# Gated layer's last two token blocks: Strassen products in the way down for five of six groups, with sums of its weights kept in DRAM

## Chip, cores and metric

One Trainium2 chip, one core. The metric is the device time of one execution in microseconds. Three runs of the kernel before took 2135.84, 2137.84 and 2135.84 us; their median is 2135.84.

## What is computed

Three layers one after another, on 4 x 576 = 2304 tokens of width 512: attention with a mask by blocks of 64 keys, a gated layer, and a layer of eight experts whose router is normalised over rows and columns in turn.

```
x = attention(q, k, v)                        # 4 batches, 8 heads, 576 tokens, 64 a head
xn = x / sqrt(mean(x*x) + 1e-6) * rms_g
g, val = xn @ w_gate, xn @ w_val              # 512 -> 1536
x = (g * sigmoid(g) * val) @ w_out            # 1536 -> 512: the way down
P = router(x)                                 # 8 rounds of row and column normalisation
out = sum over e of P[:, e] * (relu(x @ w1[e]) @ w2[e])
```

## The kernel before

**Numbers.** A float32 operand is held as two fp32r tiles, its rounded value and the rest; a product takes three matmuls (`THREE`, line 1234: high by high, high by low, low by high). A weight tile `w` is [128, 2, 512] for that reason, 512 KB. `W` (line 418) is a ring of nine of them; a tile is loaded over an old one when the last product on the old one is through.

**Blocks.** The tokens stand in five blocks, 512, 512, 512, 384, 384 wide (`BL`). `moe1` (line 1347) interleaves blocks 0, 1 and 2 of the gated layer with attention (`groups`): a group `g` is 256 of the 1536 inner columns, and there are six. Block 0 turns the raw weights into pairs and writes them to DRAM (`kept`); later blocks load those.

**Blocks 3 and 4** are the function `middle` (line 1618). They are treated as the two halves of a Strassen-Winograd scheme: `up` (line 1522) makes the gate, then the value, of a group with seven products in place of eight, each six matmuls of 384 columns. For that it needs sums and differences of quarters of two weight tiles, which `fold` (line 1328) makes: two `join`s (high plus low, 512 columns), four additions of 256 columns, and for each of two results a copy and a subtraction that split it again. For nine of twelve pairs (`PRE`, line 1322) this is done while block 2 runs and the two results go to DRAM (`folded`); the other three are folded inside `middle`. `gate` and `val` (lines 1610, 1627) apply the gate; `val` also splits its result into a pair.

**The way down** is `moe1_down` (line 1301): for each of the two blocks four products, one for each 128 output columns, each of 2 x 3 matmuls into a fresh bank of the ring `DN` (three PSUM banks). VectorE adds a bank into the accumulator `accb` (line 1318; in group 0 ScalarE copies, line 1315). The two weight tiles come by line 1640.

**Order.** Nothing is issued directly: every step is an `Op` of a `Graph` with engine, estimated duration and buffers. `emit` (line 136) lists them by a planner: a forward pass by priority, `ROUNDS` backward and forward passes, then random changes of keys (`move`) by the seeds in `MOVES`, and a last forward pass. A step with `alts` goes to the engine that the planner expects to end first, with a `margin` against the second choice. `replay` places filler matmuls (line 88) where it expects PE to be idle. The result is one fixed order for each engine; SP's is the order of the DMA issues.

## Time and profile before

| | before |
|---|---|
| median of three runs | 2135.84 us |
| the profiled execution's own time | 2134.63 us |
| its span | 2132.8 us |
| PE busy | 2110.2 us, 99% |
| VectorE (DVE) busy | 1514.5 us, 71% |
| GpSimd (POOL) busy | 1172.3 us, 55% |
| ScalarE (ACT) busy | 969.3 us, 45% |
| DMA | 414.39 MB, mean 194 GB/s |

How to read it: times are microseconds unless marked ns, counted from the span's start. PE is the matmul engine, PEld its weight loads, SP the queue that issues DMAs. A table by stretches gives for each engine the busy time and, after x, the number of instructions, then PE's granted clock as a share, the share of time in which the DMA engines were busy, and GB/s. A row of a group of instructions reads: line, engine, operation, tile written and tiles read (buffer numbers left out), shapes, count; then the busy time in all and the mean ns of one; then the idle time of the engine just before them and who ended it. A row of waits gives who waited for whom, the total, how many times, and the longest. A row of the timeline gives start and length of a merged run of like instructions. Matmuls overlap, so the distance from start to start, not the length, is the time of one. Filler matmuls and other full float32 matmuls leave two records for each instruction.

### The profile page before, as it was taken

The numbers are of one execution on the slowest core, as the hardware profiler recorded it, in microseconds if no ns is written. First come the engines' busy times: TensorE is split into PE (matmuls) and PEld (weight loads), VectorE is DVE, ScalarE is ACT, GpSimd is POOL, SyncE is SP. The second block draws the span as 40 slices with busy tenths as digits, with TensorE's granted clock in tenths as the row PEclk, the third lists the DMA queues.
The fourth block names the chain that finished last, engine by engine and source line by source line (L and its number), as shares of the span: only waits on it lengthen the run. The fifth ranks groups of instructions, "written<-read, shape, count | busy, mean of one in ns | idle before, by whom it ended". The sixth has DMA issues, their size and how long they took to land.

```text
span 2132.8 us, 31222 instructions
## 1 busy us (share of the span) xinstructions
PE 2110.2 (99%) x10810; PEld 1821.8 (85%) x10810; DVE 1514.5 (71%) x2643; ACT 969.3 (45%) x2098; POOL 1172.3 (55%) x1073
## 2 busy tenths in 40 slices
PE   9899999999999999999999999999999999999999
PEld 7678778888999999999999999999888888888887
DVE  8889887878567875655555555555767776777777
ACT  6679776664435433333433433443433233332332
POOL 5476524677447755555555555553656464564644
PEclk9999999999999999999999999999999999999999
DMA  6678855567654655554454444444656556565553
GB/s 188 183 210 257 277 169 185 187 220 247 208 177 148 230 190 185 193 183 178 179 181 179 178 178 178 178 178 168 242 203 215 182 196 213 191 217 191 196 202 113
DMA packets 168834, 414.39 MB, mean 194 GB/s; under 512 B 28298, under 2 KB 63562, under 8 KB 168676
## 3 DMA queue, kind: packets, MB, share of 16 engines
q1 hardware_dynamic: 168676, 412.39, 57.1%
q8 instruction: 85, 1.39, 0.3%
q14 instruction: 73, 0.60, 0.1%
HBM read 261.24 MB, written 150.53 MB: 193 GB/s over the span
## 4 chain that ended last, share of the span: by engine, by line
PE 90%; DVE 5%; ACT 2%; DMA 1%; POOL 1%; issue 1%; SPq 0%; DVEq 0%; POOLq 0%; ACTq 0%
PE pm L94 53%; PE ps L94 30%; PE po L94 5%; DVE mn L739 1%; PE ps L98 1%; ACT p L746 1%; DVE ptl L928 0%; DVE qa L665 0%; DMA w<-kg 0%; ACT pth L927 0%; DVE acc L1318 0%; DVE acc L506 0%; DVE xx L894 0%; DMA rd<-acc 0%; DVE ka L450 0%
## 5 line engine op out<-in xcount | busy, mean ns | idle before, releaser
L94 PE MATMUL ps<-xs,w 128*128 128x384 f32 (+2 forms) x2613 | 527.9, 345 | 0.0
L94 PEld LDWEIGHTS ps<-xs,w 128*128 128x128 f32 x2613 | 459.5, 188 | 43.5 <-ACT w L446 0.6
L94 PE MATMUL pm<-x,w 128*128 128x512 f32 (+2 forms) x1743 | 420.2, 375 | 1.0 <-POOL x L459 1.0
L94 PEld LDWEIGHTS pm<-x,w 128*128 128x128 f32 x1743 | 305.7, 189 | 50.1 <-POOL x L459 1.3
L1832 DVE SCALAR_TENSOR_TENSOR acc<-pm,Pm,acc 128x512 f32<-128x512 f32 x280 | 209.8, 750 | 130.1 <-PE pm L94 129.9
L459 POOL TENSOR_TENSOR w<-raw,w 128x512 fp32r<-128x512 f32 (+1 forms) x150 | 195.4, 1307 | 171.1 <-ACT w L446 150.8
L94 PE MATMUL pm<-w,h 128*128 128x512 f32 x1152 | 279.8, 391 | 0.0
L94 PE MATMUL pm<-h,w 128*128 128x512 f32 (+1 forms) x1068 | 248.8, 378 | 0.2 <-ACT x L446 0.2
L94 PEld LDWEIGHTS pm<-w,h 128*128 128x128 f32 x1152 | 210.1, 188 | 39.4
L94 PEld LDWEIGHTS pm<-h,w 128*128 128x128 f32 x1068 | 194.1, 188 | 29.9 <-issue 0.6
L94 PE MATMUL pm<-w,x 128*128 128x512 f32 x768 | 187.8, 392 | 0.0
L1550 DVE TENSOR_TENSOR pad<-ps,pad 128x384 f32<-128x384 f32 (+2 forms) x154 | 81.3, 528 | 142.2 <-ACT pad L1545 92.4
L94 PEld LDWEIGHTS pm<-w,x 128*128 128x128 f32 x768 | 142.8, 188 | 26.5
L94 PE MATMUL pm<-xs,w 128*128 128x256 f32 (+2 forms) x699 | 146.9, 334 | 0.0
L1956 DVE TENSOR_TENSOR acc<-pm,acc 128x512 f32<-128x512 f32 x169 | 115.8, 686 | 43.7 <-PE pm L94 40.1
L1545 ACT ACTIVATE pad<-ps 128x384 f32<-128x384 f32 (+2 forms) x142 | 68.3, 481 | 163.7 <-PE ps L94 159.3
L459 POOL TENSOR_TENSOR x<-pad,x 128x512 fp32r<-128x512 f32 (+1 forms) x68 | 95.4, 1405 | 75.8 <-ACT x L446 75.8
L94 PEld LDWEIGHTS pm<-xs,w 128*128 128x128 f32 x699 | 119.9, 189 | 14.2
L446 ACT ACTIVATE w<-raw 128x512 fp32r<-128x512 f32 (+1 forms) x184 | 107.5, 589 | 49.3 <-DMA raw<-w_dram 13.3
L94 PE MATMUL ps<-x,w 128*128 128x256 f32 (+1 forms) x627 | 114.2, 303 | 0.0
L459 POOL TENSOR_TENSOR h<-pad,h 128x512 fp32r<-128x512 f32 (+1 forms) x49 | 66.0, 1352 | 67.1 <-ACT h L446 63.1
L94 PEld LDWEIGHTS ps<-x,w 128*128 128x128 f32 x627 | 97.7, 190 | 1.8 <-issue 0.8
(385 smaller groups left out, 3794.9 us busy)
## 6 DMA issues: line engine op xcount, KB each, us to landing
raw<-w_dram SPq DMA_DIRECT2D x128, 256.0 KB, 3.3
w<-ko SPq DMA_DIRECT2D x36, 512.0 KB, 4.7
w<-kv SPq DMA_DIRECT2D x33, 512.0 KB, 4.6
fa<-w SPq DMA_DIRECT2D x32, 512.0 KB, 2.6
fc<-w SPq DMA_DIRECT2D x32, 512.0 KB, 2.7
fd<-w SPq DMA_DIRECT2D x32, 512.0 KB, 5.0
sb<-w SPq DMA_DIRECT2D x32, 512.0 KB, 4.0
sd<-pad SPq DMA_DIRECT2D x32, 512.0 KB, 2.7
```

Of the source, the lines that this page charges most:

```text
L94: return self.tensor.matmul(**k)
L98: return self.tensor.transpose(**k)
L446: nc.scalar.activation(out=out_(), in_=in_(), func=AF.Copy, scale=scale)
L459: eng.tensor_tensor(out=out_(), in0=a(), in1=b(), op=ALU.subtract)
L739: return A("DVE", t_v1(n), lambda: nc.vector.tensor_reduce(out=m()[a:z, col : col + 1], in_=ps()[a:z, o : o + n], axis=AX, op=ALU.max, neg ...
L746: A("ACT", t_act(n, True, 2), lambda: nc.scalar.activation(out=p()[a:z, c0 : c0 + n], in_=ps()[a:z, o : o + n], func=AF.Exp, bias=m()[a:z, ...
L1545: G.op("ACT", t_act(n, True), lambda: nc.scalar.activation(out=t()[:, 0:n], in_=bank()[:, 0:n], func=AF.Copy), r=[bank], w=[t])
L1550: G.op("DVE", t_v1(n), lambda: nc.vector.tensor_tensor(out=t()[:, 0:n], in0=bank()[:, 0:n], in1=t()[:, 0:n], op=ALU.add), r=[bank, t], w=[t])
L1832: G.op("DVE", 63 + t_v1(512), lambda y=y, dst=dst, tt=tt, e=e: nc.vector.scalar_tensor_tensor(out=dst(), in0=wide(y()), scalar=Pm()[:, tt, ...
L1956: G.op("DVE", t_v1(N), lambda: nc.vector.tensor_tensor(out=dst(), in0=bank()[:, 0:N], in1=dst(), op=ALU.add), r=[bank, dst], w=[dst])
```

## The change

Five parts, with lines of the kernel before.

1. `PRE` now holds all twelve pairs, so no fold is left in `middle`.
2. For groups 0 to 4 the way down takes seven products in place of eight (`down3`), each in two tiles of 128 output columns and three matmuls of 384. Products go in the order 0, 1, 5, 4, 6, 2, 3 into three banks X, Y, Z; a bank that has been read out is not cleared but takes the next product on top, and VectorE adds each reading into the accumulator it belongs to: 14 readings a group. Group 5 keeps `moe1_down`.
3. The right operands are sums and differences of the four results of a group (`operands_h`: four differences, seven splits into pairs, where before four results were split). They stand in a ring of seven (`hl`), and the way down of a group is put after the value of the next.
4. The sums of the down weights are folded while block 1 runs and written to DRAM (`put`, ten tiles); `ld` loads four tiles for a group's way down, one of them half.
5. The planner's constants (`ROUNDS` 14 to 8, `RATE` 260 to 300, smaller margins in `fold`) and the table `MOVES` are new, and with them the order of all engines throughout.

```diff
-ROUNDS = 14
+ROUNDS = 8
-MARGIN, LAND, RATE = 0.0, 2000.0, 260.0
+MARGIN, LAND, RATE = 0.0, 2000.0, 300.0
 MOVES = (
-    21000002, 21000013, 21000024, 21000031, 21000032, 21000033, 21000062, 21000067, 21000082, 21000086, 21000126,
+    34000023, 34000042, 34000043, 34000044, 34000058, 34000071, 34000078, 34000127, 34000149, 34000151, 34000155,
...
-    PRE = {('g', 1), ('g', 4), ('g', 0), ('g', 3), ('v', 2), ('g', 2), ('v', 1), ('g', 5), ('v', 0)}
+    LAST = NF // 2 - 1
+    PRE = {(a, g) for a in "gv" for g in range(NF // 2)}
...
-    def fold(w0, w1_, rr, prio):
+    def fold(w0, w1_, rr, prio, down=False):
...
-        add(256, a22, a21, a22, r=[r1], w=[r1], **k)
-        add(256, a21, a11, a21, op=ALU.subtract, r=[r0, r1], w=[r1], **k)
-        add(256, a11, a22, a11, op=ALU.subtract, r=[r0, r1], w=[r0], **k)
-        add(256, a12, a12, a11, op=ALU.subtract, r=[r0], w=[r0], **k)
+        a12, a21 = (y, x) if down else (x, y)
+        for out, a, b, op in ((a22, a21, a22, ALU.add), (a21, a11, a21, ALU.subtract), (a11, a22, a11, ALU.subtract), (a12, a12, a11, ALU.subtract)):
+            add(256, out[0], a[0], b[0], op=op, r=[*{id(z[1]): z[1] for z in (out, a, b)}.values()], w=[out[1]], prio=prio, margin=300.0)
...
+                if j == 1 and g < LAST:
+                    put("o", g, fold(*pend[3], [RAW.next(), RAW.next()], 0.5, down=True))
...
+        def operands_h(h):
...
+            (b11, b12), (b21, b22) = h
+            ops = {0: split(b11), 1: split(b21)}
+            t1 = diff(DTB.next(), b12, b11)
+            t2 = diff(DTB.next(), b22, t1)
+            ops[5], ops[4] = split(t2), split(t1)
+            ops[6] = split(diff(b12, b22, b12))
+            ops[2] = split(b22)
+            ops[3] = split(diff(t2, b21, t2))
+            return ops
+
+        def down3(g, ops):
+            wa, wb, wc, wd = (ld(b, cols) for b, cols in (
+                (kept["o", 2 * g], -256), (kept["o", 2 * g + 1], 512), (folded["o", g, 0], 512), (folded["o", g, 1], 512)))
+            wts = {0: (wa, 0), 1: (wb, 0), 3: (wb, 256), 4: (wd, 256), 5: (wc, 0), 6: (wc, 256), 2: (wd, 0)}
...
+            for dt in range(2):
+                X, Y, Z = DN.next(), DN.next(), DN.next()
...
+                for i, bank, new, (d, half) in ((0, X, True, (0, 0)), (1, Y, True, (0, 0)), (5, X, False, (0, 1)), (4, Z, True, (1, 1)),
+                                                (6, X, False, (1, 1)), (2, Z, False, (0, 1)), (3, X, False, (1, 0))):
+                    m(i, dt, bank, new)
+                    dst = accb[3 + half][2 * d + dt]
...
+                        G.op("DVE", t_v1(384), lambda dst=dst, bank=bank: nc.vector.tensor_tensor(
+                            out=dst(), in0=bank()[:, 0:384], in1=dst(), op=ALU.add), r=[bank, dst], w=[dst])
...
-                hs = up(2, 0, xm, wsv, CTB, val)
-                wos = []
-                for f in (2 * g, 2 * g + 1):
...
+                h = up(2, 0, xm, weights0("v", g, None), VTB, val)
+                if late_:
+                    down3(*late_)
+                if g == LAST:
...
+                else:
+                    late_ = (g, operands_h(h))
```

**On PE, in blocks 3 and 4.** Before, a piece of the way down of one group: two weight tiles `w3`, `w4`, two pairs `h0`, `h2`, each bank `pm` filled by 2 x 3 matmuls and then read out (`ps` is a bank of `up`).

```order
L94 MATMUL pm0_89<-h0_78,w3_69 128x384 x3
L94 MATMUL pm0_89<-h2_80,w4_70 128x384 x3
L94 MATMUL pm1_90<-h0_78,w3_69 128x384 x3
L94 MATMUL pm1_90<-h2_80,w4_70 128x384 x3
L94 MATMUL ps2_95<-xs2_5155,w8_74 128x384 x6
L94 MATMUL pm2_91<-h0_78,w3_69 128x384 x3
L94 MATMUL pm2_91<-h2_80,w4_70 128x384 x3
L94 MATMUL pm0_89<-h0_78,w3_69 128x384 x3
L94 MATMUL pm0_89<-h2_80,w4_70 128x384 x3
```

Now, the end of the way down of group 4: every bank is written by three matmuls at a time, and `pm1` (X) comes back after one or two other products.

```order
L94 MATMUL pm1_90<-h0_78,w8_74 128x384 x3
L94 MATMUL pm0_89<-h3_81,w2_68 128x384 x3
L94 MATMUL pm2_91<-h1_79,w0_66 128x384 x3
L94 MATMUL pm1_90<-h2_80,w1_67 128x384 x3
L94 MATMUL pm0_89<-x0_84,w2_68 128x384 x3
L98 MATMUL po0_96<-ident_58,raw0_75 128x128 x4
L94 MATMUL pm1_90<-x0_84,w1_67 128x384 x3
L94 MATMUL ps0_93<-xs0_5328,w5_71 128x384 x6
L94 MATMUL pm1_90<-x0_84,w0_66 128x384 x3
L94 MATMUL ps1_94<-xs1_5329,w5_71 128x384 x6
```

Each run of three is now a product of its own, read out by VectorE before the next run on that bank; some of `up`'s runs of six (or the first ones of the next layer) stand between.

**On SP, in blocks 3 and 4.** Before, the loads of about one group: `kg`, `kv`, `ko` are kept weights of gate, value and way down, `ug`, `uv` their stored sums; 128x2x256 is half a tile.

```order
L1598 DMA w5_71<-ug3_0_210 128x1024
L1598 DMA w3_69<-kg6_176 128x1024
L1598 DMA w0_66<-uv2_1_209 128x1024
L1640 DMA w1_67<-ko4_174 128x1024
L1598 DMA w4_70<-kg7_178 128x2x256
L1598 DMA w6_72<-ug3_1_211 128x1024
L1598 DMA w7_73<-kv6_177 128x1024
L1598 DMA w8_74<-kv7_179 128x1024
L1640 DMA w3_69<-ko7_181 128x1024
L1598 DMA w6_72<-ug4_0_212 128x1024
L1598 DMA w4_70<-kg8_182 128x1024
```

Now, one group: `uo` are the stored sums of the down weights.

```order
L1610 DMA w7_73<-kv6_177 128x1024
L1610 DMA w5_71<-ug3_0_220 128x1024
L1610 DMA w6_72<-ug3_1_221 128x1024
L1610 DMA w8_74<-kv7_179 128x2x256
L1610 DMA w3_69<-ko5_175 128x1024
L1610 DMA w2_68<-ko4_174 128x2x256
L1610 DMA w1_67<-uv3_1_223 128x1024
L1610 DMA w0_66<-uv3_0_222 128x1024
L1610 DMA w6_72<-kg8_182 128x1024
L1610 DMA w4_70<-uo2_0_196 128x1024
L1610 DMA w5_71<-uo2_1_197 128x1024
L1610 DMA w7_73<-kg9_184 128x2x256
```

A group's ten loads have become twelve, over the same nine tiles `w0` to `w8`.

**On PE, at the start of the second layer's second pass.** Before, the rows round the filler (line 88, operand `ident`):

```order
L94 MATMUL ps0_93<-xs0_5153,w0_66 128x512 x6
L94 MATMUL ps1_94<-xs1_5154,w0_66 128x512 x6
L94 MATMUL pm3_92<-xs0_5153,w4_70 128x512 x6
L88 MATMUL ps2_95<-ident_58 128x128 x11
L94 MATMUL ps2_95<-xs4_5157,w1_67 128x512 x6
L94 MATMUL ps0_93<-xs5_5158,w1_67 128x512 x6
L94 MATMUL pm3_92<-xs5_5158,w5_71 128x512 x6
```

Now:

```order
L94 MATMUL ps0_93<-xs0_5328,w8_74 128x512 x6
L94 MATMUL ps1_94<-xs1_5329,w8_74 128x512 x6
L94 MATMUL pm3_92<-xs0_5328,w3_69 128x512 x6
L88 MATMUL ps2_95<-ident_58 128x128 x17
L94 MATMUL ps2_95<-xs4_5332,w0_66 128x512 x6
L94 MATMUL ps0_93<-xs5_5333,w0_66 128x512 x6
L94 MATMUL pm3_92<-xs5_5333,w4_70 128x512 x6
```

The same products stand on both sides; the filler went from 11 to 17 instructions.

## Rows read from the trace of the kernel before

**Rows 1.** The page, parts 1 and 4.

```profile
PE 2110.2 (99%) x10810; PEld 1821.8 (85%) x10810; DVE 1514.5 (71%) x2643; ACT 969.3 (45%) x2098; POOL 1172.3 (55%) x1073
...
PE 90%; DVE 5%; ACT 2%; DMA 1%; POOL 1%; issue 1%; SPq 0%; DVEq 0%; POOLq 0%; ACTq 0%
```

**Rows 2.** Busy time by stretches: early, then to and in blocks 3 and 4.

```profile
0.00:480.00 480.00, 461.95 (x2362) 373.07 (x2363) 410.15 (x915) 345.16 (x857) 276.23 (x263) 1.00 0.66 208
480.00:520.00 40.00, 40.00 (x183) 33.29 (x182) 32.86 (x52) 14.85 (x30) 29.59 (x29) 1.00 0.67 224
520.00:558.00 38.00, 38.00 (x213) 34.10 (x213) 29.89 (x48) 20.08 (x43) 28.07 (x28) 1.00 0.75 263
558.00:627.00 69.00, 69.00 (x400) 69.00 (x399) 37.95 (x68) 22.63 (x45) 21.76 (x23) 1.00 0.56 184
```

**Rows 3.** PE's waits from 0 to 520 us, the longest in total.

```profile
PE ps L94 <- DVE mn L739: 2.5, 5, 0.8
PE ps L94 <- DVE qb L806: 1.4, 1, 1.4
PE pm L94 <- DVE qb L803: 1.4, 2, 1.0
```

**Rows 4.** Timeline of PE in blocks 3 and 4: start, length, instruction, count.

```profile
589.50 1.20 PE L94 MATMUL ps<-xs,w 128*128 128x384 f32 x6
590.54 1.20 PE L94 MATMUL pm<-xs,w 128*128 128x384 f32 x6
591.58 0.68 PE L94 MATMUL ps<-x,w 128*128 128x384 f32 x3
```

**Rows 5.** Timeline of PE at the start of the second pass.

```profile
1514.45 1.53 PE L94 MATMUL pm<-xs,w 128*128 128x512 f32 x6
1515.82 2.62 PE L88 MATMUL ps<-ident 128*128 128x128 f32 x22
1518.19 3.02 PE L94 MATMUL ps<-xs,w 128*128 128x512 f32 x12
```

**Rows 6.** Line 1598, the loads of gate and value weights in blocks 3 and 4.

```profile
DMA to landing us min/median/max: 3.1/3.9/6.7
```

**Rows 7.** Line 1640, the loads of down weights in blocks 3 and 4.

```profile
DMA to landing us min/median/max: 4.1/5.1/5.2
```

**Rows 8.** Busy time by stretches, two with much DMA traffic.

```profile
200.00:240.00 40.00, 39.54 (x201) 32.35 (x200) 37.06 (x85) 29.92 (x77) 24.65 (x20) 1.00 0.76 272
460.00:480.00 20.00, 20.00 (x109) 16.90 (x108) 13.26 (x36) 11.82 (x29) 15.27 (x14) 1.00 0.86 287
```

**Rows 9.** Groups of VectorE's instructions, 560 to 628 us.

```profile
L1318 DVE TENSOR_TENSOR acc<-pm,acc 128x384 f32<-128x384 f32 x22 | 12.2, 556 | 7.2 <-PE pm L94 7.0
```

**Rows 10.** Groups of GpSimd's instructions, 560 to 628 us: a fold's steps.

```profile
L1426 POOL TENSOR_TENSOR raw<-w 128x512 f32<-128x512 f32 x3 | 3.9, 1303 | 2.5 <-DMA w<-kv 2.5
L1426 POOL TENSOR_TENSOR raw<-raw 128x256 f32<-128x256 f32 x4 | 3.1, 788 | 0.3
L1426 POOL TENSOR_TENSOR raw<-raw,raw 128x256 f32<-128x256 f32 x4 | 2.9, 737 | 0.3
L459 POOL TENSOR_TENSOR w<-raw,w 128x512 fp32r<-128x512 f32 x2 | 2.6, 1293 | 1.9 <-PE pm L94 1.2 <-ACT w L446 0.7
```

**Rows 11.** Groups of VectorE's instructions, 0 to 520 us: a fold's steps.

```profile
L459 DVE TENSOR_TENSOR w<-raw,w 128x512 fp32r<-128x512 f32 x7 | 5.7, 823 | 0.7 <-ACT w L446 0.6
...
L1426 DVE TENSOR_TENSOR raw<-raw,raw 128x256 f32<-128x256 f32 x1 | 1.1, 1133 | 0.0
...
L1426 DVE TENSOR_TENSOR raw<-raw 128x256 f32<-128x256 f32 x1 | 1.0, 969 | 0.0
L1426 DVE TENSOR_TENSOR raw<-w 128x512 f32<-128x512 f32 x1 | 0.7, 684 | 0.0
```

**Rows 12.** The chain that ended last, 470 to 530 us: start, length, what.

```profile
489.49 34.10 PE pm L94 x150
```

**Rows 13.** SP's waits from 0 to 520 us: attention's loads behind GpSimd.

```profile
SPq L628 <- POOL kb L459: 23.9, 10, 8.3
```

More of the change, by code (lines that the diff above doesn't have):

```diff
@@ L330 @@
 MOVES = (
[7 rows of a table removed]
[11 rows of a table added]
 )
-SPAN = 4008
+SPAN = 4116
 def transfers(dur):
@@ L1350, in moe1, with put @@
         HALF = 5
+        def put(name, g, ws):
+            for i, w in enumerate(ws):
+                kt = scr.tile([128, 2, 512], F32, name=f"u{name}{g}_{i}")
+                folded[name, g, i] = fixed(kt)
+                G.op("SP", 1900, lambda w=w, kt=kt: nc.sync.dma_start(out=kt, in_=f32(w())), r=[w], w=[folded[name, g, i]], prio=1.5, lat=2000)
         def groups(j, gs, **k):
@@ L1616, in gate, with split @@
-            return t1
+                out=to()[:, 0:n], in0=t1()[:, 0:n], scalar=1.0, in1=src()[:, 0:n], op0=ALU.add, op1=ALU.mult), r=[t1, src], w=[to])
+            return to
+        hl = []
+        def split(x):
+            ht = hl[0].next()
+            o = lambda c: lambda: ht()[:, c, 0:384]
+            copy(G.op, 384, o(0), lambda: x()[:, 0:384], r=[x], w=[ht], margin=300.0)
+            minus(G.op, 384, o(1), lambda: x()[:, 0:384], lambda: f32(o(0)()), r=[x, ht], w=[ht], margin=300.0)
+            return ht
@@ L1618, in middle @@
         def middle(pend):
-            downs = [pend]
+            late_ = None
             for g in range(NF // 2):
-                wsg = weights0("g", g, [b.next() for b in (RB, RB)])
-                gs = up(2, 0, xm, wsg, CTB, gate)
-                for d_ in downs:
-                    moe1_down(*d_, ring=DN)
+                gs = up(2, 0, xm, weights0("g", g, None), CTB, gate)
+                if not g:
+                    moe1_down(*pend, ring=DN)
+                    hl.append(ring_of(order4() + [two(xt0, 1152 + 768 * i, 384) for i in range(3)],
+                                      [set(b.users) for b in HT[-4:]] + [x1t[4].before] * 3))
@@ L1642, in middle @@
-                downs = [(3 + half, g, [hs[0][half], hs[1][half]], wos) for half in range(2)]
+                    return t1
+                h = up(2, 0, xm, weights0("v", g, None), VTB, val)
+                if late_:
+                    down3(*late_)
+                if g == LAST:
+                    hs = [[split(t) for t in row] for row in h]
+                    wos = [ld(kept["o", f], 512) for f in (2 * g, 2 * g + 1)]
+                    for half in range(2):
+                        moe1_down(3 + half, g, [row[half] for row in hs], wos, ring=DN)
+                else:
+                    late_ = (g, operands_h(h))
```

83 lines of the change are left out of this document (46 added, 37 removed), and 16 rows, old and new, of the table MOVES.

## The prediction

> **What bounds the kernel now.** I read the page first, then the busy time by stretches, then the PE's waits, and after that single rows of the places that the change touches. The page shows PE busy for 2110.2 of 2132.8 us and on 90% of the chain that ended last [rows 1]. The table by stretches [rows 2] splits that. From 0 to 480 us, where attention runs beside the first blocks of the gated layer, PE is idle for 18.1 us (480.00 less 461.95) and VectorE is busy 410.15 of 480. From 480 us on PE never stops: the last two blocks (520 to about 665 us) show PE busy for the whole of every stretch, with VectorE at 37.95 of 69.00 and GpSimd at 21.76 in the steady part. So in the stage that the change rewrites, time is the number of products and nothing else; in the stretch before it, time is also the waits of [rows 3], the longest of them for VectorE's row maxima (2.5 us in 5 waits), which are small and many.
>
> **Products removed.** Before, a group of the way down takes 4 x 2 x 3 matmuls for each of two blocks, 48; now it takes 7 products x 2 column tiles x 3 = 42. Five groups save 30, and the two orders agree: 2136 matmuls of 384 columns, now 2106. Six of them follow each other at 589.50, 590.54 and 591.58 us [rows 4], so one costs 1.04 / 6 = 0.173 us, and 30 cost 5.2 us. They stand on the path, since PE has no gap there. **-5.2 us.**
>
> **What must cover them.** VectorE now adds 14 results of a group into the accumulators where it (or ScalarE) took 8, and forms operands. Between the first gate and the last value of the stage its order holds 203 instructions instead of 153. At 0.555 us each (12.2 us over 22) [rows 9] the 50 are 28 us in some 140, where VectorE had 67.8 of 107 us busy in the last two stretches of [rows 2]: it goes from 63% to about 84%. That is below PE, so I cost it at nothing; if that cover were gone it would show as waits of PE for VectorE's additions, because one PSUM bank now takes four products in turn and each must be read out before the next.
>
> **Loads.** A group now loads twelve weight tiles in place of ten, and 5.5 MB in 21.8 us (126 x 0.173) is 252 GB/s, against 184 GB/s in the steady part before [rows 2]. The trace has moved 272 and 287 GB/s over 40 and 20 us [rows 8], so the rate is possible and near the top. What counts is the distance on PE between the last product that reads a tile and the first that reads what is loaded over it. Counted in the orders it was never under 33 matmuls (5.7 us) and at most 6.5 us for 6 of 54 loads; now it goes down to 27 (4.7 us), and 34 of 70 loads have 39 matmuls (6.8 us) or fewer. The loads landed 3.1 to 6.7 us after issue, median 3.9 [rows 6], those of the old down weights 4.1 to 5.2 [rows 7]. At the median of 3.9 nothing is late, and 5.1 us reaches only the three shortest distances: 0. With one landing of 6.7 us in each of five groups at a distance near 5, PE loses some 1.7 us five times: 8.5. I take **+0.5 us**, near the lower end, because most landings are below the shortest distance, and not zero, because the denser bursts lengthen landings. A gain is excluded, since PE has no gap there to close.
>
> **Sums of weights.** Three folds leave the stage (the value weights of groups 3 to 5) and eight stand before it: those three, and five of the down weights. The three gone cost PE nothing where they were (GpSimd was busy 21.76 of 69 [rows 2]), so they give nothing back. One fold is two additions of 512 columns, four of 256, two copies and two subtractions of 512: on GpSimd 2 x 1.30 + 4 x 0.76 + 2 x 1.29 = 8.2 us [rows 10]. The new order sends much of it to VectorE: 33 more additions of 256 columns and 19 more subtractions of 512 than before. VectorE took 0.969 and 1.133 us for the two of 256 that it had, 0.684 for one of 512 and 0.823 for seven subtractions [rows 11]. The lower bound takes half of 0.684 for a 256: 33 x 0.34 + 19 x 0.684 = 24 us. The upper one is 33 x 1.133 + 19 x 0.823 = 53 us. VectorE has 70 us idle from 0 to 480 [rows 2], so even the upper bound fits, and after attention's last product PE still has 34.10 us of block 2 to do [rows 12]. Added also are 16 writes of 512 KB on SP's queue, behind which attention's loads stand; SP has already waited 23.9 us there for GpSimd [rows 13]. What all this does to PE before 520 us no row tells. The order of that stretch is new throughout, so a gain is as possible as a loss: between -6 us (a third of PE's 18.1 us idle) and +10 us (below). I take **0**: the heads stand at nearly the same places among PE's other products (the last one's at 403 us of PE work before and after), and the filler matmuls ahead of 160 us of PE work number 28, before 29.
>
> That a 256-column sum took longer than a 512-column one on VectorE [rows 11] has a rule beside it in the Trainium skill, "SBUF — State Buffer", section "Who interferes with whom": a VectorE instruction with two SBUF inputs and a GpSimd instruction that reads SBUF exclude each other, and the later one waits for the whole of the earlier. The trace agrees (0.969 and 1.133 us against 0.684). By that rule the folds on VectorE cost the upper 53 us, not 24, and the sum would be that of the first rival below; by the lower duration it stays as here.
>
> **Fillers.** Where the second layer's second pass begins, PE runs 22 filler records in 2.37 us, 1515.82 to 18.19 [rows 5]; they are 11 instructions, and the new order has 17 there. They run whatever happens: 6 x 2.37 / 11 = **+1.3 us**.
>
> **Sum.** -5.2 + 0.5 + 0 + 1.3 = -3.4 us. The profiled execution took 2134.63 us (span 2132.8), so it would be 2131.2; the median of the three runs is 2135.84, 1.2 us above it, and from that **2132.4 us** is forecast, 0.16% less. About 0.2%, 4.3 us, is what a measurement of this kernel can tell from no change: below 2131.6 is faster, above 2140.1 slower. The sum's own range, with loads between 0 and 3 us and the early stretch within 3 either way, is 2129 to 2138.
>
> **Rivals.**
> *The folds slow attention (slower).* VectorE carries the upper 53 us in a stretch where it is already 85% busy [rows 2], and where PE's longest waits are for VectorE [rows 3]. Its instructions run in order, so a sum that is blocked stands ahead of a row maximum. If a third of the 29 us between the two bounds reaches PE, that is +10: 2142 us. It decides once over 8 us reach PE. For it: VectorE's share. Against it: PE has other products to do, and 34 us of them at the end.
> *The early stretch comes out shorter.* The whole order before 520 us is new; PE idles 18.1 us in it. If a third goes, with the sum otherwise: 2126 us. For it: only that waits there are many and short [rows 3], the kind that an order can move. Against it: more work on VectorE, not less.
> *Loads bind the last two blocks.* At the upper bound, 8.5 us in place of 0.5, 2140 us; with half of it, 2136. Against it: a median landing below every distance. For it: half of the loads now have little to spare.
> *The products go, the time stays.* The bank that takes four products waits for VectorE each time: at 1 us a group this gives 5 us back, 2137 us. Against it: between two uses of a bank the order puts other products of about 1 us, and an addition takes 0.555 [rows 9].
>
> **How the numbers follow.** Sum as worked out, 0.48; shorter early stretch, 0.26; slowed attention, 0.12; loads bind, 0.09; products go and time stays, 0.05. Faster by over 0.2%: all of the second and four tenths of the first, 0.46. Slower: attention, and half of the loads' case, 0.17. Within: the rest, 0.37. The forecast lies within, just above the bound. The range of 8 in 10 runs from 2122 (the second case, with more than a third) to 2140 (loads at their bound); left out are the slowed attention and the far end of the second case, under 2 in 10. The likeliest case's own range stands above.
>
> **What would show it.** In the changed profile, PE's down products should number 30 fewer in five groups and the stage from the first folded product to the second layer be some 5 us shorter, with PE at the full width of every stretch and VectorE near 84%. Waits of PE for weight loads inside the stage show the third rival, waits for VectorE's additions the fourth. PE's idle time from 0 to 480 us tells the first two apart: above 26 us is the first, under 13 the second. The filler should be 34 records, 3.7 us. I am wrong if the stage is not shorter, or if the early stretch moves by more than the products save.

## The result: slower, and where the profile after shows it

The changed kernel took 2151.53 us (median of 4 runs, 2150.16 to 2153.26) beside 2136.39 for the kernel before (4 runs, 2135.84 to 2137.84): ratio 1.007, 95% interval 1.0053 to 1.0088. That is 15 us more, outside the predicted range and on its far side. The profiled execution took 2152.8 us, its span is 2151.0.

The page of the changed kernel answers to [rows 1]: its first part (busy time of each engine) and the shares of the chain that ended last.

```profile
PE 2120.3 (99%) x10790; PEld 1820.5 (85%) x10790; DVE 1574.5 (73%) x2731; ACT 976.0 (45%) x2112; POOL 1216.1 (57%) x1101
...
PE 87%; DVE 7%; ACT 2%; DMA 2%; issue 1%; POOL 1%; SPq 0%; DVEq 0%; ACTq 0%; POOLq 0%
```

PE has fewer instructions and is busy 10.1 us longer, and its share of the chain fell from 90 to 87%. The changed kernel's busy time by stretches, the same as in [rows 2] and the two that follow:

```profile
0.00:480.00 480.00, 459.81 (x2301) 365.16 (x2302) 411.50 (x932) 342.79 (x848) 283.34 (x266) 0.98 0.67 211
480.00:520.00 40.00, 40.00 (x193) 33.48 (x192) 32.13 (x65) 14.12 (x28) 28.50 (x26) 1.00 0.81 278
520.00:558.00 38.00, 37.53 (x191) 31.10 (x190) 31.17 (x54) 19.40 (x41) 26.61 (x24) 1.00 0.86 303
558.00:627.00 69.00, 67.20 (x384) 65.95 (x383) 53.99 (x104) 29.63 (x63) 24.07 (x23) 1.00 0.77 249
627.00:680.00 53.00, 53.00 (x310) 51.58 (x309) 45.20 (x95) 23.35 (x57) 26.33 (x32) 1.00 0.63 209
680.00:700.00 20.00, 17.48 (x107) 14.97 (x106) 15.58 (x28) 10.20 (x25) 16.22 (x22) 0.91 0.36 126
```

Read the column behind the five engines too. From 0 to 480 us PE idles 20.2 us (480 less 459.81), only 2.1 more than before, but the mean granted clock is 0.98 and not 1.00. The trace shows 6.83 us at half clock (1.2 GHz in place of 2.4) from 23.95 us and 10.24 us from 112.69; before there was one such piece in this stretch, 3.41 us. A matmul at half clock counts as busy, and so does a filler, so neither loss stands in the idle time. To see all of it at once I took from the trace the distance from each matmul's start to the next. What is over columns / 2.4 GHz + 13 ns is lost: that is 173 ns for 384 columns, as in [rows 4], and 226 for 512, where the usual distance in this trace is 227. Of a filler the whole distance is lost. Half of the time at half clock is set apart. The lines add up to the span of each profiled execution:

| us | before | changed | difference |
|---|---|---|---|
| products, at the close distance | 2015.0 | 2009.8 | -5.2 |
| lost at full clock, 0 to 500 us | 103.8 | 107.4 | +3.6 |
| lost at full clock, 500 to 700 us | 6.3 | 12.7 | +6.3 |
| lost at full clock, from 700 us | 15.7 | 20.0 | +4.3 |
| half clock | 1.7 | 9.9 | +8.2 |
| start, end, short matmuls that come closer | -9.7 | -8.8 | +0.9 |
| span | 2132.8 | 2151.0 | +18.1 |

This pair makes the clock's part too large: the profiled execution before had a mean clock of 0.999 and this one 0.995, while all runs had 0.9971 and 0.9962. Between the means of all runs lie 14.0 us, and only about 1.3 of them go with the clock (by the fit under "Experiments"). The lines at full clock hold without that: the last two blocks and their end, 500 to 700 us, lose more than the removed products give.

The changed kernel's longest waits of PE from 0 to 520 us, which answer to [rows 3]:

```profile
PE ps L98 <- ACT p L750: 4.7, 6, 2.3
PE ps L94 <- DVE qb L810: 3.4, 2, 2.5
PE po L94 <- DVE ptl L932: 1.7, 5, 0.7
PE ps L94 <- DVE acc L890: 1.7, 2, 1.4
```

The longest was 1.4 us before (in a wait for `qb`) and is 2.5 now. And the whole list from 520 to 800 us, where the same view of the kernel before lists no wait at all:

```profile
PE po L98 <- ACT raw L1271: 2.1, 1, 2.1
PE pm L94 <- DMA w<-uv: 1.1, 1, 1.1
PE pm L94 <- DVE acc L1897: 1.0, 1, 1.0
PE po L94 <- DVE lg L1280: 0.9, 2, 0.5
PE ps L94 <- DMA w<-ug: 0.7, 1, 0.7
```

Two are for loads of weights inside the stage (1.8 us together, at 584 and 595 us). The one of 2.1 us and one of the two for `lg` are at its end; the other `lg` is at 539 us, and `acc` at 764, in the layer of experts.

**A wait beside attention, and the clock behind it.** The changed kernel's timeline from 108 us, all engines:

```profile
108.41 1.40 POOL L463 TENSOR_TENSOR qa<-rq,qa 64x576 fp32r<-64x576 f32 x1 [0.22 <-ACT qa L450]
...
108.70 1.19 DVE L1150 SCALAR_TENSOR_TENSOR tm<-xx,rgs,ss 128x64 f32<-128x64 f32 x1
...
109.81 0.67 DVE L1299 SCALAR_TENSOR_TENSOR t<-t,pm 128x512 f32<-128x512 f32 x1
...
111.12 0.21 DVE L810 TENSOR_TENSOR qb<-ps,acc 10x64 fp32r<-10x64 f32 x1
...
111.39 0.50 PE L94 MATMUL ps<-qa,ka 128*128 128x512 f32 x1 [2.51 <-DVE qb L810]
```

A VectorE product of 64 columns takes 1.19 us and ends right after GpSimd's operation does, at 109.81 (in e_early below, where it stands later, it takes 0.27); another stands behind it, and only then come the row maxima for which PE stops 2.51 us. Busy time in the 10.20 us right behind, first of the changed kernel:

```profile
112.70:122.90 10.20, 9.66 (x23) 6.48 (x24) 6.92 (x16) 1.92 (x6) 1.71 (x1) 0.50 0.34 119
```

and of the kernel before:

```profile
112.70:122.90 10.20, 9.23 (x44) 7.29 (x43) 10.00 (x16) 5.43 (x12) 7.30 (x6) 1.00 0.46 141
```

At 0.50 of the clock (1.2 GHz) PE starts 23 matmuls where it started 44; the order is another, but the columns tell the same (8,000 against 17,856). This is no accident of one execution: in all ten profiled executions with the changed kernel's order (this one and the e_, l_ and s_ runs below on the changed kernel) a piece at half clock begins between 108 and 113 us, in eight of them 10.24 us long and in two 3.41. The kernel before and l_before have none there. No new sum of weights runs yet: the first step of one is at 244 us.

**A wait behind a sum of weights.** The changed kernel's timeline at 397 us, all engines:

```profile
396.71 1.42 POOL L463 TENSOR_TENSOR kb<-rq,ka 64x576 fp32r<-64x576 f32 x1 [5.69 <-ACT ka L450]
...
397.02 2.96 DVE L669 SCALAR_TENSOR_TENSOR qa<-rq,qa 64x576 fp32r<-64x576 f32 x1
...
398.09 3.02 POOL L1433 TENSOR_TENSOR raw<-w 128x512 f32<-128x512 f32 x2
...
400.23 0.67 ACT L750 ACTIVATE p<-ps,mn 128x512 f32<-128x512 f32 x1
...
401.04 0.55 PE L98 MATMUL ps<-ident,p 128*128 128x128 f32 x3 [2.30 <-ACT p L750]
```

VectorE's product, which waited for the GpSimd operation at 396.71, ends only at 399.98, after the first of the two at 398.09 as well; it took 2.96 us, the other 18 of its kind 0.75 to 0.92. An exponential waits for what stands behind it, and PE 2.30 us for that.

The two GpSimd operations are the first steps of a sum of weights, but not of a new one: the writes of the new sums of down weights were issued from 261.0 to 364.8 us. The same place in e_mid (below) names the tile, a kept gate weight `kg`, and the gate weights' sums are all in the old `PRE` too:

```profile
398.64 1.53 POOL L1439 TENSOR_TENSOR raw<-w 128x512 f32<-128x512 f32 x1 [0.22 <-DMA w<-kg]
...
400.11 0.55 PE L98 MATMUL ps<-ident,p 128*128 128x128 f32 x3 [2.30 <-ACT p L756]
```

s_none below, which leaves out the additions of the down weights, keeps the product at 2.96 us and the wait at 2.30. The kernel before has such a product too, 2.78 us at 412.51, and PE waited 1.12 us behind it. So this stop is the order's and not the new sums'.

**The end of the last two blocks.** PE's timeline in the changed kernel from 680 us:

```profile
681.51 4.56 PE L94 MATMUL pm<-h,w 128*128 128x384 f32 x24
688.18 0.55 PE L98 MATMUL po<-ident,raw 128*128 128x128 f32 x3 [2.10 <-ACT raw L1271]
689.14 1.17 PE L94 MATMUL po<-acc,gwr 128*32 128x384 f32 x8 [0.42 <-DVE lg L1280]
690.24 4.65 PE L94 MATMUL ps<-xs,w 128*128 128x384 f32 x18
```

and, from its timeline of all engines, two rows between the first and the second of these:

```profile
684.63 0.73 POOL L1433 TENSOR_TENSOR pad<-raw 128x256 f32<-128x256 f32 x1
...
687.65 0.47 ACT L1271 ACTIVATE raw<-po 128x384 f32<-128x384 f32 x1
```

PE has nothing to do after the last product of the way down: the first sums of weights of the 8-expert layer begin on GpSimd at 684.63 us, and the copy of the logits comes at 687.65. Half clock follows from 689.55, 3.41 us. In the kernel before the same products flowed on without a gap:

```profile
670.19 4.46 PE L94 MATMUL pm<-h,w 128*128 128x384 f32 x24
674.49 0.49 PE L98 MATMUL po<-ident,raw 128*128 128x128 f32 x3
674.74 1.30 PE L94 MATMUL ps<-xs,w 128*128 128x384 f32 x6
```

From the start of the last product of the way down to that of the first one of the next layer (`ps<-xs`) it is 0.42 us there and 4.50 now.

### The profile page after: what moved, and what is told of

It is laid out like the page before. It is cut to its first block, busy times and chain, and to the rows that moved or that the text cites. A ratio compares the mean times of both kernels' runs of the same rounds, so it can differ in the third digit from the quotient of the medians.

```text
span 2151.0 us, 31416 instructions
## 1 busy us (share of the span) xinstructions
PE 2120.3 (99%) x10790; PEld 1820.5 (85%) x10790; DVE 1574.5 (73%) x2731; ACT 976.0 (45%) x2112; POOL 1216.1 (57%) x1101
## 4 chain that ended last, share of the span: by engine, by line
PE 87%; DVE 7%; ACT 2%; DMA 2%; issue 1%; POOL 1%; SPq 0%; DVEq 0%; ACTq 0%; POOLq 0%
PE pm L94 51%; PE ps L94 30%; PE po L94 5%; DVE mn L743 1%; PE ps L98 1%; ACT p L750 1%; DVE ptl L932 1%; DVE qa L669 0%; ACT p L915 0%; DMA w<-uv 0%; POOL pad L1433 0%; DVE xx L898 0%; DVE acc L1322 0%; DVE xx L994 0%; DMA w<-ug 0%
## 5 line engine op out<-in xcount | busy, mean ns | idle before, releaser
L94 PE MATMUL ps<-xs,w 128*128 128x384 f32 (+2 forms) x2685 | 545.5, 345 | 0.7 <-DMA w<-ug 0.7
L94 PEld LDWEIGHTS ps<-xs,w 128*128 128x128 f32 x2685 | 474.9, 188 | 47.3 <-DMA w<-ug 1.0
L94 PE MATMUL pm<-x,w 128*128 128x512 f32 (+2 forms) x1809 | 434.9, 373 | 1.1 <-DMA w<-uv 1.1
L463 POOL TENSOR_TENSOR w<-raw,w 128x512 fp32r<-128x512 f32 (+1 forms) x142 | 181.0, 1276 | 142.4 <-ACT w L450 137.5
L94 PE MATMUL pm<-h,w 128*128 128x512 f32 (+1 forms) x948 | 231.4, 385 | 0.2 <-ACT x L450 0.2
L94 PEld LDWEIGHTS pm<-h,w 128*128 128x128 f32 x948 | 174.5, 189 | 32.6 <-DMA w<-ko 1.0
L94 PE MATMUL pm<-xs,w 128*128 128x512 f32 (+2 forms) x723 | 152.8, 334 | 0.0
L450 ACT ACTIVATE w<-raw 128x512 fp32r<-128x512 f32 x196 | 115.5, 591 | 73.5 <-DMA raw<-w_dram 52.4
L463 POOL TENSOR_TENSOR w<-pad,w 128x512 fp32r<-128x512 f32 x64 | 87.3, 1381 | 80.7 <-ACT w L450 77.7
L1433 POOL TENSOR_TENSOR pad<-raw,raw 128x256 f32<-128x256 f32 x64 | 48.1, 751 | 80.8 <-DMA raw<-w_dram 80.8
```

The lines of the kernel that those rows point to most:

```text
L94: return self.tensor.matmul(**k)
L450: nc.scalar.activation(out=out_(), in_=in_(), func=AF.Copy, scale=scale)
L463: eng.tensor_tensor(out=out_(), in0=a(), in1=b(), op=ALU.subtract)
L1433: eng.tensor_tensor(out=out_(), in0=a(), in1=b(), op=op)
```

## Experiments

The time of one kernel changes from run to run with the mean granted clock: in the 63 runs of the kernel before beside these experiments it went from 2134.61 us at 0.999 to 2140.84 at 0.995, a fitted 1.6 us for each 0.001, taken as 1.5. So beside each ratio stands a corrected difference: the mean time less 1.5 us for each 0.001 of clock below 1, less the same of those 63 runs. For the changed kernel it is +12.7 us (mean clock 0.9962 against 0.9971); the standard error of each is 0.2 to 1.0, so two of them differ by chance by 1 us or more. The correction takes out the clock that a kernel's own stops cost it, too.

| kernel | median us | ratio to before, 95% | corrected |
|---|---|---|---|
| changed | 2151.53 | 1.0070 (1.0053 to 1.0088) | +12.7 |
| e_early | 2149.98 | 1.0064 (1.0047 to 1.0081) | +11.9 |
| e_mid | 2153.84 | 1.0076 (1.0063 to 1.0090) | +12.7 |
| e_exit | 2148.90 | 1.0055 (1.0041 to 1.0069) | +10.4 |
| e_all | 2149.10 | 1.0057 (1.0043 to 1.0071) | +10.7 |
| t_before | 2130.71 | 0.9963 (0.9950 to 0.9976) | -4.9 |
| t_after | 2153.45 | 1.0071 (1.0054 to 1.0088) | +15.6 |
| t_sums | 2157.33 | 1.0088 (1.0071 to 1.0106) | +20.5 |
| t_plain | 2150.22 | 1.0056 (1.0041 to 1.0071) | +13.9 |
| l_both | 2145.42 | 1.0035 (1.0022 to 1.0048) | +8.0 |
| l_before | 2136.95 | 1.0001 (0.9991 to 1.0010) | 0.0 |
| l_early | 2151.17 | 1.0068 (1.0052 to 1.0083) | +12.5 |
| l_mid | 2144.45 | 1.0036 (1.0021 to 1.0051) | +7.5 |
| x_before | 2137.99 | 0.9997 (0.9987 to 1.0006) | -1.7 |
| x_after | 2152.15 | 1.0066 (1.0049 to 1.0083) | +10.4 |
| x_after2 | 2156.50 | 1.0083 (1.0068 to 1.0098) | +15.8 |
| x_after_mid | 2143.76 | 1.0026 (1.0017 to 1.0035) | +4.4 |
| s_none | 2146.66 | 1.0045 (1.0033 to 1.0057) | +9.9 |
| s_none_mid | 2147.48 | 1.0047 (1.0033 to 1.0061) | +8.4 |

### Mending single places of the order

Theory A: the loss sits in a few places of this order. Rival B: the load. Each edit moves a few operations in the finished order; nothing else changes.

```
         fills = self.replay(order)
+        for ops, behind in SHIFT:
+            ops = [self.ops[i] for i in ops]
+            order = [o for o in order if o not in ops]
+            at = order.index(self.ops[behind]) + 1
+            order[at:at] = ops
...
+SHIFT = (([1136, 1137, 1155], 1135), ([3339], 3225), ([4505], 4497), ([4461], 4451))
```

e_early has the first entry, e_mid the second, e_exit the last two, e_all all four.

> One place of the changed kernel's order is mended, nothing else: on VectorE the two writes of qb (the row maxima and the copy) for which TensorE waits 2.5 us and 0.7 us at 109 to 113 us go ahead of the two operations that stand before them now (a product of 1.19 us that waits there behind a GpSimd operation, and one of 0.67). Theory A (the loss sits in a few places where the new order has an operation that TensorE needs stand behind another in its queue, and in the half clock that follows such a stop): the wait falls to about 1 us, the 10.2 us at half clock at 112.7 us are gone, and the run is 4 to 7 us shorter than the changed kernel (2145 to 2147.5). Rival B (the load: VectorE, GpSimd and the transfers have too much beside the products, so that a mended wait comes back a little later): no more than 1.5 us shorter (2150 or more).

> One exchange in the changed kernel's order: on VectorE the short minimum of the row maxima goes ahead of the product of rq that stands 2.96 us at 397 us while GpSimd does two sums of the new down weights; the exponential that TensorE waits 2.3 us for at 398.7 us hangs on that minimum. Theory A: the wait falls from 2.3 us to 0.5 or less, the run is 1.5 to 2.5 us shorter (2149 to 2150). Rival B: another operation is caught behind the same sums, less than 0.5 us gained. The clock did not fall after this stop, so nothing more is to be had.

> Two exchanges on ScalarE where the last two blocks end (684 to 690 us): the copy of the logits, for which TensorE waits 2.1 us at 686.1 us, and the rounding of the first sums of weights of the 8-expert layer go ahead of two evictions. Theory A: the stop of 2.1 us is cut to some 0.6 us and one of about 1 us, the products of the first pass begin 1 to 1.5 us earlier (688.7 to 689.2 instead of 690.2), and if the clock then stays up the 3.4 us at half clock give back another 1.7: 1 to 3 us shorter. Rival B: the sums of weights on GpSimd, which begin only when the last differences are done, hold the first products anyway: under 0.5 us.

> All three mended places in one kernel. Theory A: the gains add, 7 to 11 us, 2140 to 2144.5, between the two kernels; what is left over the kernel before (4 to 8 us) is the half clock at 24 us (6.8 us), the waits for loads at 580 to 600 us and the many small gaps. Rival B: 0 to 3 us in all.

A was wrong for two of the three places. In e_early the wait moved, as PE's rows in its timeline show:

```profile
109.72 0.50 PE L94 MATMUL ps<-qa,ka 128*128 128x512 f32 x1 [0.91 <-DVE qb L816]
...
112.64 0.79 PE L94 MATMUL ps<-ka,qa 128*128 128x512 f32 x1 [1.76 <-ACT p L831]
```

0.91 + 1.76 us stand where 2.51 + 0.66 stood: ScalarE's exponential, which frees the next PSUM bank, had its own queue. Of the half clock 3.41 us remained in that execution, but all 10.24 in e_all's, which has the same edit. In e_mid PE still waited 2.30 us, because a copy of the qa that VectorE makes late stands ahead of the exponential on ScalarE. e_exit did gain 2.3 us (corrected): PE's two waits there are 0.60 and 0.84 us, and the half clock behind them is gone in both executions with this edit (e_exit, e_all; of the eight without, seven have it). All three together gave 2 us, not 7 to 11. The queues of three engines are late together in these places; one exchange doesn't free them.

### Other orders, and the parts of the change apart

To tell the order from the change, four variants got a table (`TABLE`) of the same kind, each from the same search with the same effort: t_before is the kernel before, t_after the changed kernel, and t_sums and t_plain leave parts of the change out. The planner's constants stay as each kernel has them (`RATE` 260 in t_before, 300 in the others, and the smaller margins).

> The kernel before with another table of key changes: 230 seeds found from an empty table by a random search that keeps a seed when the planner's own replay gets shorter, with VectorE, ScalarE and GpSimd some per cent slower and transfers a little slower than the planner assumes. The same search, of the same length, was made for the changed kernel (t_after) and two mixtures. Theory A (what was lost is the order that the changed kernel's table gives): t_after lies 2 to 6 us under t_before, as the products say. Theory B (the change itself takes room from VectorE, GpSimd and the transfers, and any order pays for it): t_after lies 4 us or more above t_before. For this kernel alone both expect 2125 to 2140.

> The changed kernel, all of it, with a table of 285 seeds from the same search as t_before. Theory A: 2 to 6 us under t_before, 2125 to 2136. Theory B: 4 us or more above t_before; still shorter than the changed kernel as it is (2151.5), by up to 10, since the search allowed for slower engines.

> The changed kernel with the way down of all groups as plain products again (48 matmuls a group, two tiles of weights), but with all the sums of weights still made and written, the five of the down weights to no use; table from the same search. It carries the sums without the saving. Theory A: t_after plus 4 to 5 us (30 products). Theory B: the sums are what costs, so t_after plus 4 to 10 and well above t_before.

> t_sums without the five sums of the down weights: the changed kernel's buffers and its twelve sums of the up weights, plain way down; table from the same search. The difference to t_sums is the price of the five sums. Theory A: 0 to 1 us. Theory B: 2 to 8 us less than t_sums. What it then still lies above t_before is the three more sums of value weights in block 2 and the rings cut smaller.

In t_sums the way down is plain again, against the changed kernel; t_plain leaves out the `put("o", ...)` of `moe1`, the sums of the down weights, as well:

```
-                if late_:
-                    down3(*late_)
...
+                hs = [[split(t) for t in row] for row in h]
+                wos = [ld(kept["o", f], 512) for f in (2 * g, 2 * g + 1)]
+                downs = [(3 + half, g, [row[half] for row in hs], wos) for half in range(2)]
```

Theory A falls: t_after lies 22.7 us above t_before in the medians, 20.4 corrected. Three readings follow, each between two kernels with different orders, so with some us of doubt. The seven products in place of plain ones: t_after less t_sums, -4.9 corrected. The five sums of down weights with their writes: t_sums less t_plain, +6.6. The rest (three more sums of value weights before the stage, its buffers, and the planner's constants): t_plain less t_before, +18.8. Busy time by stretches (the first number behind the comma is PE's), first of t_before:

```profile
100.00:200.00 100.00, 97.40 (x478) 77.69 (x478) 83.42 (x180) 80.97 (x195) 70.64 (x62) 1.00 0.67 208
200.00:500.00 300.00, 299.59 (x1541) 248.27 (x1540) 244.53 (x568) 205.38 (x523) 166.46 (x148) 1.00 0.67 221
660.00:700.00 40.00, 40.00 (x235) 35.77 (x235) 33.15 (x69) 23.44 (x55) 30.70 (x36) 1.00 0.57 202
```

then of t_sums:

```profile
100.00:200.00 100.00, 95.67 (x467) 73.47 (x466) 87.26 (x190) 81.43 (x198) 63.37 (x57) 0.98 0.61 185
200.00:500.00 300.00, 292.54 (x1468) 238.08 (x1467) 260.15 (x575) 207.25 (x521) 166.55 (x147) 0.99 0.71 228
660.00:700.00 40.00, 38.59 (x249) 36.45 (x248) 28.97 (x59) 19.31 (x53) 23.47 (x32) 1.00 0.24 83
```

and of t_plain:

```profile
100.00:200.00 100.00, 95.40 (x475) 74.60 (x474) 91.76 (x198) 84.63 (x210) 68.53 (x60) 1.00 0.70 212
200.00:500.00 300.00, 297.74 (x1510) 244.50 (x1510) 251.85 (x565) 203.42 (x511) 145.80 (x126) 1.00 0.69 223
660.00:700.00 40.00, 36.96 (x235) 32.90 (x234) 32.23 (x72) 20.66 (x57) 24.85 (x30) 0.96 0.28 97
```

From 200 to 500 us, where the down weights are summed, PE idles 0.4 us in t_before, 2.3 in t_plain and 7.5 in t_sums. From 660 to 700 us it never stops in t_before, and stops 1.4 and 3.0 us in the two with the changed stage. t_plain and t_sums have the plain way down, so that stop is not the seven products'.

The idle time misses the fillers here too. The same account as above, for these executions and for the orders of the next but one section (x_):

| us | before | t_before | x_before | changed | t_after | x_after | x_after2 | t_sums | t_plain |
|---|---|---|---|---|---|---|---|---|---|
| products | 2015.0 | 2015.0 | 2015.0 | 2009.8 | 2009.8 | 2009.8 | 2009.8 | 2015.0 | 2015.0 |
| lost, 0 to 500 us | 103.8 | 98.6 | 95.4 | 107.4 | 108.6 | 103.0 | 102.8 | 110.9 | 102.8 |
| lost, 500 to 700 us | 6.3 | 6.3 | 6.4 | 12.7 | 14.0 | 13.6 | 17.2 | 16.4 | 19.2 |
| lost, from 700 us | 15.7 | 16.8 | 18.7 | 20.0 | 20.6 | 20.7 | 24.8 | 18.7 | 17.8 |
| half clock | 1.7 | 3.3 | 11.7 | 9.9 | 8.3 | 11.6 | 6.6 | 3.3 | 1.6 |

Early, one order differs from another by as much as the kernels do. From 500 to 700 us it doesn't: the three orders with the old stage lose 6.3 or 6.4 us, the six with the new one 12.7 to 19.2. Of the 16.6 us between t_plain's execution and t_before's, 12.9 lie there (8.2 us of fillers in t_plain, none in t_before) and 4.2 before. What the six share is more than the products: weights that all come by loads, operands spread over three slots of the rings in `slots` in place of two (`sides`), a ring of eight temporaries split into six and three (`CTB`, `VTB`), and one of four cut to three (`CT0`). Which of these makes the difference was not tried; for the loads see the next section.

### Transfers

Theory C: loads land later than the new plan (300 GB/s in place of 260) counts on. The order stays; the transfers move a quarter of the columns.

```
-            G.op("SP", 1900 if cols == 512 else 950, lambda: nc.sync.dma_start(out=f32(w()[:, :, o:z]), in_=b()[:, :, o:z]),
+            e = o + (z - o) // 4
+            G.op("SP", 1900 if cols == 512 else 950, lambda: nc.sync.dma_start(out=f32(w()[:, :, o:e]), in_=b()[:, :, 0 : e - o]),
```

That is l_mid; l_early cuts the load in `Loader.get` to `[:, :, 0:128]`, l_both and l_before cut all loads and writes of the gated layer's weights and sums.

> The changed kernel with its order untouched, but every write of a weight tile of the gated layer to DRAM, every write of a sum of weights and every load of either back moves a quarter of the columns (the products read what an earlier tile left in the rest, so the result is another; the same instructions run in the same order). Theory C (transfers: the changed kernel's plan counts on 300 GB/s and on loads that land early; they land later, operands come late, and the queues behind them stand): most of the 15 us are gone, 2131 to 2139, and l_both lies within 4 us of l_before. Theory B (the sums and additions on VectorE and GpSimd): at most 4 us gained, 2147 or more, and still 10 us or more above l_before.

> The kernel before with the same cut: its writes and loads of the gated layer's weights and sums move a quarter of the columns. Theory C: 0 to 4 us less than before (2132 to 2136), since its plan left the transfers room. Theory B: the same, 0 to 3 us less.

> The changed kernel where only the loads of kept weights for blocks 0 to 2 (beside attention) move a quarter of the columns; writes, and the loads of the last two blocks, are whole. Theory C: the part of the loss that lies from 100 to 500 us, 6 to 10 us less (2142 to 2146). Theory B: under 2 us.

> The changed kernel where only the loads in the last two blocks move a quarter of the columns. Theory C: the late weights at 580 to 600 us are gone, and the stop at the end of the stage is shorter: 3 to 6 us less (2145.5 to 2148.5). Theory B: 2 to 3 us (the late weights alone).

C holds in part in the last two blocks and nowhere else: l_mid is 5.2 us under the changed kernel (corrected), l_early 0.2, l_both no better than l_mid, so most of the 15 us stay. The stop at the end of the stage, which C had shorter, is 2.10 us in l_mid as before. How long the stage's loads took in the changed kernel (line 1610; 27 of 70 loads have a landing on record):

```profile
DMA to landing us min/median/max: 3.2/4.6/6.2
```

and with a quarter of the columns, in l_mid (line 1611 there):

```profile
DMA to landing us min/median/max: 2.2/2.6/3.5
```

And l_mid's busy time in the steady part, where PE had 67.20 of 69.00 us in the changed kernel:

```profile
558.00:627.00 69.00, 69.00 (x400) 68.92 (x399) 57.72 (x113) 31.64 (x67) 23.67 (x24) 1.00 0.24 67
```

The waits for `uv` and `ug` are gone. They were 1.8 us. From 500 to 700 us l_mid, l_both and s_none_mid (below), which all have the short loads there, lose 10.0, 10.0 and 10.1 us at full clock against 12.7: the traces give the loads 2.6 us of the 5.2, and the rest isn't pinned to rows. With short loads the stage still loses 3.7 us more than in the kernel before.

### The best order found, and the sums' arithmetic

> The kernel before with its order written out: a longer search for it (with transfers at 265 to 272 GB/s and VectorE 4 to 7% slower than planned, values with which the planner's replay puts the six orders measured so far in their measured sequence), then the list of all operations as it came out. Both theories: 2125 to 2131, a little under t_before.

> The changed kernel with its order written out, from the same search, as long. Theory A (order alone): at or under the kernel before, 2128 to 2136, and within 4 us of x_before. Theory D (two parts: some of the 15 us are this order's, the rest the change's own price: sums of weights beside attention, loads in the last two blocks, PE dry where that stage ends): 2136 to 2144, 8 to 14 us above x_before.

> The changed kernel with an order written out that was searched from a plan with 260 GB/s in place of 300 (as before the change) and that the planner's replay finds nearly indifferent to slower transfers. If loads that land later than planned are what hurts the changed kernel's orders, it lies 3 us or more under x_after; if not, level with it or up to 4 us above.

> x_after with the loads of the last two blocks cut to a quarter of their columns (the products read what an earlier tile left; the result is another), as l_mid did with the changed kernel's own order. Theory D: 2 to 5 us under x_after. Theory A: under 2 us.

In these four the list of operations takes the place of the table, `for n in LINE: o = self.ops[n >> 2]; o.eng, o.dur, o.fn = o.alts[n & 3]`. One caution first: x_before gives another result than the kernel before (relative error 0.023), which was not meant, and why is not known. So its time is a hint and no more. That the change loses came out again: x_after is 12.1 us above x_before and 15.3 above t_before (corrected). But x_after is only 2.3 under the changed kernel as it was (0.6 above it in the medians), and x_before gained 1.7 on the kernel before: both came out longer than either theory expected. x_after2, whose order should hardly mind late transfers, lies 5.4 above x_after: early transfers beside attention aren't the matter, as l_early said. x_after_mid gives the loads of the stage 6.0 us under another order; from 500 to 700 us its trace loses 9.7 us at full clock against x_after's 13.6, which is 3.9.

> The changed kernel in its own order, without the 30 additions and subtractions of the five sums of down weights (two of 512 columns and four of 256 for each; what is rounded and written to DRAM is what an earlier tile left, so the result is another). All transfers, all products and every other operation stay. Theory D (the change's own price has the sums in it, as t_sums less t_plain, 7 us, says): 3 to 7 us less than the changed kernel, 2144.5 to 2148.5. Theory A (the order alone): under 2 us.

> s_none and l_mid in one: neither the additions of the five sums nor three quarters of each load in the last two blocks. Theory D: the two prices add, 9 to 14 us less than the changed kernel (2137.5 to 2142.5); what is then left over the kernel before, with 30 products less, is the order's and the end of the stage. Theory A: as l_mid, 2143 or more.

```
+        if down:
+            G.skip |= set(G.ops[n0:])
...
-            o.fn()
+            if o not in self.skip:
+                o.fn()
```

Without the 30 additions the changed kernel is 4.9 us shorter in the median and 2.8 corrected, just under the lower edge, with an error of about 1; its trace loses 106.8 us at full clock from 0 to 500 us against 107.4. The prices didn't add: s_none_mid lies 4.3 under the changed kernel, no lower than l_mid alone. So some us of the stage and of the sums are the same us: where one wait goes, another operation is next.

## Why the prediction was wrong

Two terms failed that the sum put at nothing or nearly so: the early stretch ("I take 0") and the last two blocks with their end (+0.5 for loads, nothing for cover).

**Products: right.** -5.2 us was predicted, and at the close distance the products of the two traces take 2015.0 and 2009.8 us. t_after less t_sums, -4.9, is between two orders whose other lines differ by up to 5 us each; that it comes so near is luck.

**Fillers: right.** 34 records were expected, 3.7 us, and the timeline of PE has them; the next matmul starts 3.71 us later:

```profile
1532.54 3.96 PE L88 MATMUL ps<-ident 128*128 128x128 f32 x34
```

**What must cover them: right inside the stage, wrong at its end.** VectorE is busy 53.99 of 69.00 us, 78%, and PE waits for none of its additions there, at 555 ns each:

```profile
L1689 DVE TENSOR_TENSOR acc<-pm,acc 128x384 f32<-128x384 f32 x30 | 16.4, 555 | 6.2 <-PE pm L94 5.8
```

But a cover ends with its stage. The sum had no term for the end: there the operands and sums of the 8-expert layer's first pass queue on VectorE and GpSimd with the last group's additions. From the start of the last product of the way down to that of the next layer's first it is 0.17 to 0.42 us in before, t_before and x_before, and 1.9 to 4.5 in all six orders with the new stage's buffers (the changed kernel, t_after, t_sums, t_plain, x_after, x_after2). With the loads, the stretch from 500 to 700 us lost 6.3 us more than before (7.9 with its half clock), where +0.5 was forecast. By the prediction's own sign, a stage some 5 us shorter, this alone makes it wrong. What in the new stage does it, beyond the loads, stays open.

**Loads: within the bounds, the wrong value.** I took +0.5 of 0 to 8.5, reasoning that the median landing of 3.9 us [rows 6] lies under every distance. The price is 2.6 (l_mid) to 3.9 us (x_after_mid) by the traces and 5.2 to 6.0 by the corrected times. It isn't that every landing grew: [rows 6] are the gate and value weights alone, and 14 of their 42 loads have a landing on record. All of the stage's loads together had a median of 4.2 us before and 4.6 after, with 6.7 and 6.2 as the longest. A median was the wrong thing to hold against the shortest distances; loads in the upper half meet them.

**Sums of weights: the early term of 0 failed, and mostly not by the sums.** From 0 to 500 us the changed kernel's execution loses 3.6 us more at full clock and 6.6 more to the half clock. From 100 to 200 us, where no sum of down weights runs yet, 5.0 us go to the clock behind the stop at 109 us. There x_after2, with the same operations, idles 2.0 us; the changed kernel idles 5.5 and the kernel before 3.9. So the order does this, as it does the stop at 398.7. What the new sums cost is less sure: 2.8 us by the times of s_none, 0.6 by its trace, 6.6 by t_sums less t_plain, with their writes and two orders. The bounds of 24 and 53 us for VectorE's part were sound: to 560 us it has 34 more sums of 256 columns and 20 more subtractions of 512 than before, which add some 32 us. But 34 of its 37 sums of 256 columns took 0.39 to 0.43 us, near the lower price, and only three 0.70 to 1.24. I had argued from places of heads and from a count of fillers that the early order was as good as before. It was not, and neither number can tell.

**The sign I named didn't work.** Over 26 us idle from 0 to 480 would have been the first rival; it was 20.2. Most of the early loss was in the clock, which my idle time left out.

The rival of slowed attention (2142 us) was nearest, but the result lies above it. Attention was slowed, though hardly by the folds; loads bound in part; and the end of the stage no rival names. I had given each rival as if it came alone. No order tried brought the change below the kernel before. The one kernel that beats both is t_before, the kernel before with another table: 2130.71 us.

## What to carry to other kernels

Removing 30 products from a kernel with 10,810 records of matmuls pays only if the engines that feed them keep their slack: price what every other engine, and the stage behind, must now do in the same time, and hold the longer landings, not the median, against the shortest distances. Where a planner's table sets the order, one order against one order mixes the change with luck of several us; compare variants with tables of equal effort. Count stops together with the granted clock behind them and the fillers put in their place, never by idle time alone.

## What the runs showed of the hardware

A VectorE operation with two SBUF inputs that waits for GpSimd can be overtaken by GpSimd's next one: the 64x576 product took 2.96 us at 397.02 and ended 1.85 us after the GpSimd operation it first waited for; alone it takes 0.755. In e_mid it took 2.84, and in the kernel before one took 2.78 at 412.51, where GpSimd's operation from 413.39 to 414.67 went ahead of it as well. The Trainium skill, "SBUF — State Buffer", section "Who interferes with whom", says that a VectorE instruction with two SBUF inputs contends with a GpSimd instruction that reads SBUF, over ports that are locked for one of them; the trace agrees (2.96 against 0.755 us). Where VectorE waited and GpSimd's next operation followed closely, GpSimd's went first in all three.

The same stop doesn't always bring the same clock. After the 2.30 us at 398.7 the clock stayed up in the changed kernel's profiled execution; in e_mid's and s_none's it fell to half for 3.41 us behind the same wait.
